# Moving the seven-product scheme from the w_out matmuls to the W matmuls, with W's blocks kept in DRAM

## Chip, cores, metric

One core of a Trainium2 chip. The metric is the device time of one execution in microseconds (us). Five engines run their own instruction queues in order: TensorE (PE; its weight loads are listed as PEld), VectorE (DVE), ScalarE (ACT), GpSimd (POOL) and SyncE (SP, which issues the DMAs here). "Wide" below means a matmul of 512 columns, "narrow" one of 256.

## What is computed

```python
# q, k, v: (4, 6080, 256); w_in: (256, 2048); w_out: (2048, 256)
qn = q / (norm(q, axis=1) + 1e-6);  kn = k / (norm(k, axis=1) + 1e-6)
s = kn.transpose(0, 2, 1) @ qn / tau          # 256 x 256 for each batch
a = softmax(s)                                # rows
x = (v @ a).reshape(24320, 256)
h = maximum(x @ w_in, 0)
out = h * h @ w_out
```

The kernel never forms x: for each batch b it makes W = a @ w_in (256 x 2048), and the output is relu(v W)^2 w_out. The inputs w_in and w_out are 64-bit floats.

## The kernel before

**Tiling.** Tokens of a batch are cut into NB = 12 blocks, ten of 512 and two of 480: 48 blocks in all, numbered (b, n). W has 2048 columns, NF = 16 slices of 128. A step is one block and one slice f; two steps are a pair (r = f // 2, part = f % 2), so a block is 8 pairs. `steps` lists them all; the first two blocks are interleaved by groups of four slices (the first PAIR = 32 steps), while weights are still decoded.

**Precision.** Every product of 32-bit numbers is made of three matmuls in a faster format: each operand is split into a high part (a cast on ACT) and a low part (a subtraction on DVE), and hi x hi, hi x lo, lo x hi are added in PSUM. So wo_hi/wo_lo hold w_out, w_hi/w_lo hold W, v_hi/v_lo a block of v, and g_hi/g_lo the squared activations.

**First product** (`first_product`, PSUM tile ps_h): for a step, 2 x 3 wide matmuls, v block by W slice, then a relu by ACT into x. It is the ordinary block product: for a pair, 12 wide matmuls, "eight products" of 2 x 2 blocks.

**Second product** (PSUM tile ps_o): from block 2 on, except for the last block, each pair uses a scheme of seven block products in place of eight (`seven_products`, 21 narrow matmuls for a pair, 9 in part 0 and 12 in part 1). It needs sums of the activations (`squares_and_sums`, on DVE), their hi and lo parts (`parts_of_sums`), sums of w_out's blocks (`sums_of_w_out`, once, tiles wS_hi/wS_lo), and at the end of a block `combine`, five DVE adds, and four output DMAs. Blocks 0, 1 and the last use `eight_products` (12 wide for a pair, evicted by ACT at the end of a block).

**The order.** The main loop runs over steps; at each it issues the first product of this step, pieces of the attention work, the square and splits of this pair or the one before, and the second product of the pair LAG = 2 pairs earlier. `InProgramOrder` keeps each engine's instructions in that order. The attention work of batches 1 to 3 is a generator (`attention`): 25 chunks of q and k a batch (five of batch 1 are done before), each split into hi and lo in one pair and multiplied into the Gram matrix in the next, then softmax, then W in four groups (`softmax_and_W`, PSUM tile ps_w). It is advanced once in each step, except in the steps f = 2 and 3. Group g of W for the next batch waits until the last block of this batch has used the old one (`may_write_W`), because W lives in SBUF (pool wpool, tags w_hi and w_lo, four buffers each, one for a group).

**PSUM.** ps_h has three buffers of one bank, ps_o two of two banks, the Gram matrix one bank.

**v.** A block of v is loaded by one DMA, cast to v_hi at f = 6 and subtracted to v_lo at f = 8 of the block before.

Of the kernel before, what the change touches and what calls it, by code (L numbers as in the profile page):

```python
# [30 lines left out]
def kernel(  # L31
# [36 lines left out]
    PPG = FPG // 2  # L68
    LAST = 3
# [44 lines left out]
    def decode(k, hi_lo, raw, shape, read):  # L114

        words = raw.bitcast(I32).rearrange("p a (b w) -> p a b w", w=2)  # L120
        low, high = words[:, :, :, 0], words[:, :, :, 1]
        E = pool.tile(shape, I32, tag=("qk_lo", "o_sb")[k % 2], name="dec_e", bufs=1)
        M = pool.tile(shape, I32, tag=("qk_hi", "dec")[k % 2], name="dec_m", bufs=1)
# [77 lines left out]
    def sums_of_w_out():  # L201
# [3 lines left out]
        for g in range(NG):  # L205
            fs, rs = slice(g * FPG, (g + 1) * FPG), slice(g * PPG, (g + 1) * PPG)
            w = pool.tile([P, FPG, C], F32, tag="qk_hi", name=f"wo{g}", bufs=1)
            S = pool.tile([P, 4, PPG, P], F32, tag="qk_lo", name=f"wo_sums{g}", bufs=1)
# [193 lines left out]
    def softmax_and_W(b):  # L402
# [41 lines left out]
        diag = pool.tile([P, NC, P], F32, tag="diag", name=f"diag{b}", bufs=1)  # L444
# [39 lines left out]
        for g in range(NG):  # L484
            while (b, g) not in may_write_W:
                yield
# [7 lines left out]
            w_hi = wpool.tile([P, NC, GRP], F32R, tag="w_hi", name=f"w_hi{b}_{g}")  # L494
            w_lo = wpool.tile([P, NC, GRP], F32R, tag="w_lo", name=f"w_lo{b}_{g}")
# [16 lines left out]
            def evict(h):  # L512
                ps = ps_w.pop(h)[:, 0:GRP]
                scalar.activation(w_hi[:, h, :], ps, AF.Copy, scale=rinv[:, h : h + 1])
# [9 lines left out]
            if b == 0:  # L524
# [3 lines left out]
                for h in range(NC):  # L528
                    evict(h)
            else:  # L530
                for h in range(NC):
# [5 lines left out]
                    yield  # L537
            W[b, g] = w_hi, w_lo
            yield
# [3 lines left out]
    may_write_W = {(0, g) for g in range(NG)}  # L543
    V = {}

# [6 lines left out]
    def split_v_hi(b, n):  # L552
        tn = blocks[n][1]
        V[b, n][1] = pool.tile([P, NC, T], F32R, tag="v_hi", name=f"v_hi{b}_{n}")
        scalar.copy(V[b, n][1][:, :, :tn], V[b, n][0][:, :, :tn])

# [4 lines left out]
    def split_v_lo(b, n):  # L561
        tn = blocks[n][1]
        raw, hi, _ = V[b, n]
        V[b, n][2] = pool.tile([P, NC, T], F32R, tag="v_lo", name=f"v_lo{b}_{n}")
        vector.tensor_sub(V[b, n][2][:, :, :tn], raw[:, :, :tn], hi[:, :, :tn].bitcast(F32))

    def by_seven(b, n):

        return (0, 1) < (b, n) < order[-1]

    X = {}
    G = {}

    def first_product(b, n, f):
        tn = blocks[n][1]
# [9 lines left out]
        if f % 2 == 0:  # L585
            X[b, n, f // 2] = pool.tile([P, 8, tn // 2], F32, tag="x", name=f"x{b}_{n}_{f // 2}")
        x = X[b, n, f // 2].rearrange("p s t -> p (s t)")
        s = slice((f % 2) * tn, (f % 2 + 1) * tn)
        scalar.activation(x[:, s], ps[:, :tn], AF.Relu)

    def parts_of(b, n, r):
        half = blocks[n][1] // 2
        shape = [P, 7 if by_seven(b, n) else 4, half]
        return [pool.tile(shape, F32R, tag=name, name=f"{name}{b}_{n}_{r}") for name in ("g_hi", "g_lo")]

    def squares_and_sums(b, n, r):

        x = X[b, n, r]  # L600
        G[b, n, r] = hi, lo = parts_of(b, n, r)
        scalar.activation(x[:, 0:4, :], x[:, 0:4, :], AF.Square)
        if by_seven(b, n):
            hi_, lo_, src = hi[:, 0:3, :], lo[:, 0:3, :], x[:, 1:4, :]
            vector.tensor_sub(x[:, 4:6, :], x[:, 1:3, :], x[:, 0:1, :].broadcast_to(list(x[:, 1:3, :].shape)))
            scalar.copy(hi_, src)
            vector.tensor_add(x[:, 6, :], x[:, 2, :], x[:, 4, :])
            vector.tensor_sub(x[:, 7, :], x[:, 3, :], x[:, 6, :])
            vector.tensor_sub(lo_, src, hi_.bitcast(F32))

    def parts_of_sums(b, n, r):

        x = X.pop((b, n, r))
        hi, lo = G[b, n, r]
        if by_seven(b, n):
            hi, lo, src = hi[:, 3:7, :], lo[:, 3:7, :], x[:, 4:8, :]
        else:
            src = x[:, 0:4, :]
# [5 lines left out]
    def second_product(b, n, r, part):  # L624
        if by_seven(b, n):
            seven_products(b, n, r, part)
        else:
            eight_products(b, n, r, part)

    def weights_of(r):  # L630

        out = {}
        for name, i, j in (("A11", 0, 0), ("A12", 0, 1), ("A22", 1, 1)):
            out[name] = [w[:, 2 * r + j, i * P : (i + 1) * P] for w in (wo_hi, wo_lo)]
        for i, name in enumerate(("S1n", "S2", "S3", "S4")):
            out[name] = [late[part][:, i, r, :] for part in ("hi", "lo")]
        return out


    SEVEN = (  # L640
        (None, ("A11", 0), ("A12", 2), ("S2", 5)),
        (("S1n", 3), ("S3", 4), ("S4", 1), ("A22", 6)),
    )

    def seven_products(b, n, r, part):
        t0, tn = blocks[n]
        half = tn // 2
        if r == 0:
            O[b, n, part] = ps_acc.tile([P, 4, T // 2], F32, tag="o", name=f"ps_o{b}_{n}_{part}")
        ps = O[b, n, part]  # L650
        hi, lo = G[b, n, r]
        w = weights_of(r)
        begun = set()
        for at, product in enumerate(SEVEN[part]):
            if product is None:
                continue
            w_hi, w_lo = w[product[0]]
            slot = product[1]
            for i, (wt, gt) in enumerate(((w_hi, hi), (w_hi, lo), (w_lo, hi))):
                tensor.matmul(  # L660
                    ps[:, at, :half],
                    wt,
                    gt[:, slot, :],
                    start=r == 0 and at // 2 not in begun,
                    stop=r == NPAIR - 1 and i == 2,
                    skip_group_check=True,
                )
                begun.add(at // 2)
        if part:
            del G[b, n, r]  # L670
        if r == NPAIR - 1:

            if part == 0:
                O[b, n] = pool.tile([P, 7, half], F32, tag="o_sb", name=f"o{b}_{n}", bufs=1)
            o, first = O[b, n], 1 - part
            scalar.copy(o[:, 3 * part : 3 * part + 4 - first, :], O.pop((b, n, part))[:, first:4, :half])
# [3 lines left out]
    def combine(b, n):  # L680
# [5 lines left out]
        vector.tensor_add(o[:, 1:3, :], o[:, 1:3, :], both(0))  # L686
        yield
        vector.tensor_add(o[:, 4, :], o[:, 4, :], o[:, 2, :])
        vector.tensor_add(o[:, 0, :], o[:, 4, :], o[:, 3, :])
        yield  # L690
        vector.tensor_add(o[:, 3, :], o[:, 3, :], o[:, 2, :])
        vector.tensor_add(o[:, 5:7, :], o[:, 5:7, :], o[:, 3:5, :])
        at = b * N + t0
        out = outT[:, at : at + tn].rearrange("(m p) t -> p m t", p=P)
        for m, k, slot in ((0, 0, 5), (0, 1, 1), (1, 0, 0), (1, 1, 6)):
# [5 lines left out]
    def eight_products(b, n, r, part):  # L701
# [4 lines left out]
        hi, lo = (x.rearrange("p s t -> p (s t)")[:, part * tn : (part + 1) * tn] for x in G[b, n, r])  # L706
# [73 lines left out]
    def then_sums():  # L780
        while grams[1].raws if B > 1 else False:
            yield
        yield from sums_of_w_out()

    sums = then_sums()
# [6 lines left out]
    LAG = 2  # L792
    beside = attention_of_others()
    for i in range(len(steps) + 2 * LAG):
        part = now["part"] = i % 2
        if i < len(steps):
# [3 lines left out]
            if n == NB - 1 and f % FPG == FPG - 1:  # L800
                may_write_W.add((b + 1, f // FPG))
# [3 lines left out]
        else:  # L805
# [5 lines left out]
            if i > 24:  # L811
# [16 lines left out]
        if i >= 2 * LAG:  # L828
            second_product(*pairs[i // 2 - LAG], part)
        if i < len(steps):  # L830
            at_hi, at_lo = (None, None) if at == 0 else (12, 13) if at == 1 else (6, 8)
            if i == 2 and len(order) > 2:
                load_v(*order[2])
            if f == at_hi and at + 1 < len(order):
                split_v_hi(*order[at + 1])
            if f == at_lo and at + 1 < len(order):
                split_v_lo(*order[at + 1])
                if at + 2 < len(order):
                    load_v(*order[at + 2])
        if i >= PAIR and part:  # L840
            for gen in gens:
                next(gen, None)

# [26 lines left out]
```

## Time and profile before

| | |
|---|---|
| median of 3 runs | 2222.92 us (2221.24 to 2222.95) |
| the profiled execution | 2223.07 us, span 2221.3 us |
| TensorE matmuls, busy | 2206.3 us (99%), 13740 instructions |
| ACT busy | 1845.8 us (83%) |
| DVE busy | 1761.8 us (79%) |
| DMA | 126.99 MB, mean 57 GB/s |
| granted TensorE clock | 0.999 |

The span is from the first to the last instruction on the core. A group line of the profile reads: line, engine, operation, output<-inputs with shapes, count | busy us, mean ns of one | idle time before it and who ended it. All helpers record one source line (L27), so instructions are told apart by tile names and shapes. A timeline line is start, duration, engine, operation, count of merged instructions, and in brackets the idle time before and who ended it. Matmul rows overlap each other, and their ends are modelled; the distance of starts is their pace.

### The profile page before, as it was taken

Reading aid. Unit: us, or ns where it says so; the run is one execution under the profiler, and the core shown is the slowest. Engines: PE = TensorE matmul, PEld = TensorE weight load, DVE = VectorE, ACT = ScalarE, POOL = GpSimd, SP = SyncE. Lnnn points to the kernel's source line nnn. Section 1 sums busy time; section 2 is a strip of 40 time slices with the busy share of each in tenths; the row PEclk is TensorE's granted clock in tenths of the full one; section 3 lists DMA queues with packets and bytes.
Section 4 is the critical chain, followed back from the end, with each engine's and each line's share of the span. In section 5 each row is a group of like instructions: output and inputs, shape, how many; then the busy total and the mean of one; then the engine's idle time right before and its main releaser. Section 6 shows DMA issues by size and latency. Waiting matters only on the chain.

```text
span 2221.3 us, 34359 instructions
## 1 busy us (share of the span) xinstructions
PE 2206.3 (99%) x13740; PEld 1980.9 (89%) x13740; DVE 1761.8 (79%) x2470; ACT 1845.8 (83%) x2294; POOL 0.7 (0%) x6
## 2 busy tenths in 40 slices
PE   8999999999999999999999999999999999999999
PEld 7788999989989999988998999998899888888898
DVE  7868888878778888878777888887877777787773
ACT  5788888888778888888878888888887888888885
POOL 0000000000000000000000000000000000000000
PEclk9999999999999999999999999999999999999999
DMA  9510122110211112110111122110102010010000
GB/s 341 178 67 29 60 69 70 47 38 25 70 66 58 60 60 72 62 41 22 36 67 56 60 66 75 58 53 22 33 25 76 21 36 20 22 37 20 22 26 18
DMA packets 76495, 126.99 MB, mean 57 GB/s; under 512 B 7728, under 2 KB 35120, under 8 KB 76336
## 3 DMA queue, kind: packets, MB, share of 16 engines
q1 hardware_dynamic: 76336, 124.81, 17.2%
q8 instruction: 107, 1.75, 0.3%
q14 instruction: 52, 0.43, 0.1%
HBM read 95.68 MB, written 29.10 MB: 56 GB/s over the span
## 4 chain that ended last, share of the span: by engine, by line
PE 95%; DVE 3%; DMA 1%; ACT 1%; issue 0%; SPq 0%; DVEq 0%; ACTq 0%
PE ps_h L27 46%; PE ps_o L27 41%; PE gram L27 5%; PE ps_w L27 2%; DVE g_lo L27 1%; DMA qk<-in_k 1%; DVE acc L27 1%; DVE x L27 0%; ACT x L27 0%; DMA qk<-in_q 0%; ACT g_hi L27 0%; PE ps_n L27 0%; DVE o L27 0%; DVE dec_m L27 0%; DVE wo_sums L27 0%
## 5 line engine op out<-in xcount | busy, mean ns | idle before, releaser
L27 DVE TENSOR_TENSOR g_lo<-x,g_hi 128x768 fp32r<-128x768 f32 (+2 forms) x744 | 804.5, 1081 | 96.2 <-ACT g_hi L27 95.7
L27 DVE TENSOR_TENSOR x<-x 128x256 f32<-128x256 f32 (+3 forms) x1080 | 551.4, 511 | 274.4 <-ACT x L27 249.3
L27 ACT CAST g_hi<-x 128x768 fp32r<-128x768 f32 (+2 forms) x744 | 697.7, 938 | 23.8 <-DVE x L27 10.5
L27 ACT ACTIVATE x<-ps_h 128x512 f32<-128x512 f32 (+1 forms) x768 | 456.7, 595 | 297.2 <-PE ps_h L27 277.3
L27 PE MATMUL ps_h<-v_hi,w_hi 128*128 128x512 f32 (+1 forms) x1536 | 478.8, 393 | 0.0
L27 PE MATMUL ps_h<-v_hi,w_lo 128*128 128x512 f32 (+1 forms) x1536 | 478.0, 392 | 0.0
L27 PE MATMUL ps_h<-v_lo,w_hi 128*128 128x512 f32 (+1 forms) x1536 | 475.2, 390 | 0.0
L27 ACT ACTIVATE x<-x 128x1024 f32<-128x1024 f32 (+1 forms) x384 | 404.6, 1054 | 11.9
L27 PE MATMUL ps_o<-g_lo,wS_hi 128*128 128x256 f32 (+1 forms) x1440 | 402.4, 279 | 3.0 <-DVE g_lo L27 2.8
L27 PE MATMUL ps_o<-g_hi,wS_lo 128*128 128x256 f32 (+1 forms) x1440 | 401.6, 279 | 0.0
L27 PE MATMUL ps_o<-g_hi,wS_hi 128*128 128x256 f32 (+1 forms) x1440 | 400.8, 278 | 0.0
L27 PEld LDWEIGHTS ps_h<-v_lo,w_hi 128*128 128x128 f32 x1536 | 288.1, 188 | 65.0
L27 PEld LDWEIGHTS ps_h<-v_hi,w_lo 128*128 128x128 f32 x1536 | 288.8, 188 | 62.1
L27 PE MATMUL ps_o<-g_hi,wo_hi 128*128 128x256 f32 (+3 forms) x1176 | 330.6, 288 | 1.0 <-ACT g_hi L27 1.0
L27 PE MATMUL ps_o<-g_hi,wo_lo 128*128 128x256 f32 (+3 forms) x1176 | 330.8, 288 | 0.0
L27 PE MATMUL ps_o<-g_lo,wo_hi 128*128 128x256 f32 (+3 forms) x1176 | 330.3, 287 | 0.1
L27 PEld LDWEIGHTS ps_o<-g_lo,wS_hi 128*128 128x128 f32 x1440 | 271.3, 188 | 19.6 <-DVE g_lo L27 3.8
L27 PEld LDWEIGHTS ps_o<-g_hi,wS_hi 128*128 128x128 f32 x1440 | 270.8, 188 | 15.5
L27 PEld LDWEIGHTS ps_o<-g_hi,wS_lo 128*128 128x128 f32 x1440 | 271.0, 188 | 0.0
L27 PEld LDWEIGHTS ps_h<-v_hi,w_hi 128*128 128x128 f32 x1536 | 239.0, 188 | 5.2
L27 PEld LDWEIGHTS ps_o<-g_hi,wo_hi 128*128 128x128 f32 x1176 | 221.5, 188 | 17.6 <-ACT g_hi L27 1.4
L27 PEld LDWEIGHTS ps_o<-g_lo,wo_hi 128*128 128x128 f32 x1176 | 220.8, 188 | 16.8 <-DVE g_lo L27 0.5
(87 smaller groups left out, 1667.9 us busy)
## 6 DMA issues: line engine op xcount, KB each, us to landing
qk<-in_k SPq DMA_DIRECT2D x87, 256.0 KB, 2.8
qk<-in_q SPq DMA_DIRECT2D x87, 256.0 KB, 3.0
v<-in_vT SPq DMA_DIRECT2D x40, 512.0 KB, 3.8
out_T<-o SPq DMA_DIRECT2D x152, 128.0 KB, 1.7
wi_hi<-wi_kept SPq DMA_DIRECT2D x12, 512.0 KB, 3.3
wi_lo<-wi_kept SPq DMA_DIRECT2D x12, 512.0 KB, 4.1
w_raw<-in_w_in SPq DMA_DIRECT2D x4, 1024.0 KB, 5.2
w_raw<-in_w_out SPq DMA_DIRECT2D x4, 1024.0 KB, 5.6
```

Of the source, the lines that this page charges most:

```text
L27: return lambda *args, **kwargs: self.tc.keep_in_program_order(issue(*args, **kwargs))
```

## The change

The seven-product scheme moves to the first product. From block 3 on (FIRST = 3) the product with W takes seven block products (`first_by_seven`), and the second product takes eight everywhere (BY_SEVEN is empty, so `some_by_seven` is false and `eight_products` runs for every block). Blocks 0 to 2 keep the ordinary first product.

`first_by_seven` holds two ps_h tiles, `one` and `two`, for a pair. In part 0 it makes four block products (12 narrow matmuls); then ACT copies `one` to SBUF, and DVE makes u, adds onto the halves `one[1]` and `two[1]` in PSUM, and makes c22. In part 1 three more block products (9 narrow) are accumulated onto `one[0]`, `one[1]` and `two[1]`, and ACT takes the relu of c22, `one` and `two[1]`. Squares and splits follow as in a block by eight; the sums on the activations, `combine` and its four DMAs are gone.

v's blocks are needed in sums too: `split_v_hi` (f = 9) and `split_v_lo` (f = 10) split three blocks of v, `sums_of_v` (f = 13) makes four sums on DVE and casts them on ACT, `parts_of_v_sums` (f = 14) makes their low part; the next v is loaded at f = 14.

W's blocks and their sums are made once a batch (`sums_of_W`; `keep_first_W` for batch 0, in the place of `sums_of_w_out`) and written to DRAM (W_kept, two sets, by b % 2). For each pair `load_W` reads the seven blocks, hi and lo, in two DMAs of 128 x 3584 bytes, AHEAD_W = 3 pairs ahead, into the buffers w_hi and w_lo. The wait may_write_W is gone.

```diff
+    BY_SEVEN = ()
+    FIRST_SEVEN = 4
...
-            while (b, g) not in may_write_W:
-                yield
...
+    def sums_of_W(b, g, w, parts=None):
+        v = w.rearrange("p j (r i m) -> p i j r m", r=PPG, i=2)
+        (A11, A12), (A21, A22) = [[v[:, i, j] for j in range(2)] for i in range(2)]
+        S = pool.tile([P, 4, PPG, P], F32, tag="qk", name=f"w_sums{b}_{g}", bufs=QK_BUFS)
+        S1, S2, S3, S4 = (S[:, i] for i in range(4))
+        vector.tensor_add(S1, A21, A22)
+        vector.tensor_sub(S3, A11, A21)
+        vector.tensor_sub(S2, S1, A11)
+        vector.tensor_sub(S4, A12, S2)
+        yield
+        if parts is None:
+            hi = pool.tile([P, NC, GRP], F32R, tag="qk_hi", name=f"w_hi{b}_{g}", bufs=1)
+            lo = w.bitcast(F32R)
+            scalar.copy(hi, w)
+            vector.tensor_sub(lo, w, hi.bitcast(F32))
             yield
+        else:
+            hi, lo = parts
+        S_hi = pool.tile([P, 4, PPG, P], F32R, tag="qk_lo", name=f"wS_hi{b}_{g}", bufs=1)
+        scalar.copy(S_hi, S)
+        vector.tensor_sub(S.bitcast(F32R), S, S_hi.bitcast(F32))
+        for i, (a, sums) in enumerate(((hi, S_hi), (lo, S))):
...
+                nc.sync.dma_start(kept[:, 0:2, :], a[:, 0, :, r, :])
+                nc.sync.dma_start(kept[:, 2, :], a[:, 1, 1, r, :])
+                nc.sync.dma_start(kept[:, 3:7, :], sums[:, :, r, :])
...
+    def load_W(b, r):
...
+        for part, kept in zip(parts, W_kept[b % 2][r]):
+            nc.sync.dma_start(part.bitcast(F32), kept)
...
+            V[b, n][1] = hi = pool.tile([P, 7, tn // 2], F32R, tag="v_hi", name=f"v_hi{b}_{n}")
+            scalar.copy(hi[:, 0, :], raw[:, 0, 0 : tn // 2])
+            scalar.copy(hi[:, 1:3, :].rearrange("p k t -> p (k t)"), raw[:, 1, :tn])
...
+    def sums_of_v(b, n):
...
+        vector.tensor_sub(T1, B12, B11)
+        vector.tensor_sub(T3, B22, B12)
+        vector.tensor_sub(T2, B22, T1)
+        vector.tensor_sub(T4n, B21, T2)
+        scalar.copy(hi[:, 3:7, :], S)
...
+        x = x_of(b, n, r)
+        if part == 0:
+            H[b, n, r] = one, two = [
+                ps_h.tile([P, 2, T // 2], F32, tag="h", name=f"ps_h{b}_{n}_{r}_{i}") for i in range(2)
+            ]
+            product(one[:, 0], 0, 0, True, False)
+            product(one[:, 1], 3, 3, False, False)
+            product(two[:, 0], 4, 4, True, False)
+            product(two[:, 1], 5, 5, False, False)
+            u, p1, p5, c22 = (x[:, i, :] for i in range(4))
+            scalar.copy(x[:, 1:3, :], one[:, :, :half])
+            vector.tensor_add(u, two[:, 0, :half], p1)
+            vector.tensor_add(one[:, 1, :half], u, p5)
+            vector.tensor_add(two[:, 1, :half], two[:, 1, :half], u)
+            vector.tensor_add(c22, two[:, 1, :half], p5)
+        else:
+            one, two = H.pop((b, n, r))
+            product(one[:, 0], 1, 1, False, True)
+            product(one[:, 1], 6, 2, False, True)
+            product(two[:, 1], 2, 6, False, True)
+            scalar.activation(x[:, 3, :], x[:, 3, :], AF.Relu)
+            scalar.activation(x[:, 0:2, :], one[:, :, :half], AF.Relu)
+            scalar.activation(x[:, 2, :], two[:, 1, :half], AF.Relu)
...
+            if part == 0 and at >= FIRST - 1:
+                ahead = at * NPAIR + f // 2 + AHEAD_W
+                if FIRST * NPAIR <= ahead < len(order) * NPAIR:
+                    load_W(order[ahead // NPAIR][0], ahead % NPAIR)
...
+            if at + 1 >= FIRST and at + 1 < len(order):
+                at_hi, at_lo = 9, 10
+                if f == 13:
+                    sums_of_v(*order[at + 1])
+                if f == 14:
+                    parts_of_v_sums(*order[at + 1])
+                    if at + 2 < len(order):
+                        load_v(*order[at + 2])
```

More of the change, by code (lines that the diff above doesn't have):

```diff
@@ L513, in evict @@
                 ps = ps_w.pop(h)[:, 0:GRP]
+                if b:
+                    scalar.activation(w[:, h, :], ps, AF.Copy, scale=rinv[:, h : h + 1])
+                    return
                 scalar.activation(w_hi[:, h, :], ps, AF.Copy, scale=rinv[:, h : h + 1])
@@ L529, in softmax_and_W @@
                     evict(h)
+                W[b, g] = w_hi, w_lo
+                yield
             else:
@@ new lines, with keep_first_W @@
+    done_W = set()
+    def keep_first_W():
+        for g in range(NG):
+            hi, lo = W[0, g]
+            w = pool.tile([P, NC, GRP], F32, tag="qk", name=f"w0_{g}", bufs=QK_BUFS)
+            vector.tensor_add(w, hi.bitcast(F32), lo.bitcast(F32))
+            yield
+            yield from sums_of_W(0, g, w, (hi, lo))
+    loaded = {}
+    def load_W(b, r):
+        assert (b, r // PPG) in done_W, (b, r)
+        loaded[b, r] = parts = [
+            wpool.tile([P, 7, P], F32R, tag=tag, name=f"{tag}{b}_{r}") for tag in ("w_hi", "w_lo")
+        ]
+        for part, kept in zip(parts, W_kept[b % 2][r]):
+            nc.sync.dma_start(part.bitcast(F32), kept)
@@ L544 @@
     V = {}
+    FIRST = 3
     def load_v(b, n, tag="v"):
@@ L562, in split_v_lo, with by_seven, some_by_seven, x_of @@
         tn = blocks[n][1]
[L563 to L569, printed above, removed]
+        raw, hi = V[b, n][:2]
+        if plain(b, n):
+            V[b, n][2] = pool.tile([P, NC, T], F32R, tag="v_lo", name=f"v_lo{b}_{n}")
+            vector.tensor_sub(V[b, n][2][:, :, :tn], raw[:, :, :tn], hi[:, :, :tn].bitcast(F32))
+        else:
+            V[b, n][2] = lo = pool.tile([P, 7, tn // 2], F32R, tag="v_lo", name=f"v_lo{b}_{n}")
+            vector.tensor_sub(lo[:, 0, :], raw[:, 0, 0 : tn // 2], hi[:, 0, :].bitcast(F32))
+            flat = lambda x: x[:, 1:3, :].rearrange("p k t -> p (k t)")
+            vector.tensor_sub(flat(lo), raw[:, 1, :tn], flat(hi).bitcast(F32))
+    def by_seven(b, n, r):
+        return (0, FIRST_SEVEN) <= (b, n) < order[-1] and r in BY_SEVEN
+    def some_by_seven(b, n):
+        return any(by_seven(b, n, r) for r in range(NPAIR))
     X = {}
+    XS = {}
     G = {}
+    def x_of(b, n, r):
+        if (b, n, r) not in X:
+            X[b, n, r] = pool.tile([P, 4, blocks[n][1] // 2], F32, tag="x", name=f"x{b}_{n}_{r}")
+        return X[b, n, r]
     def first_product(b, n, f):
+        if plain(b, n):
+            first_by_eight(b, n, f)
+        else:
+            first_by_seven(b, n, f // 2, f % 2)
+    def first_by_eight(b, n, f):
         tn = blocks[n][1]
@@ L598, in squares_and_sums @@
     def squares_and_sums(b, n, r):
         x = X[b, n, r]
[L601 to L609, printed above, removed]
+        shape = [P, 4, blocks[n][1] // 2]
@@ new lines, in squares_and_sums @@
+        G[b, n, r] = [pool.tile(shape, F32R, tag=name, name=f"{name}{b}_{n}_{r}") for name in ("g_hi", "g_lo")]
+        hi, lo = G[b, n, r]
+        scalar.activation(x, x, AF.Square)
+        if by_seven(b, n, r):
+            hi, lo, src = hi[:, 1:4, :], lo[:, 1:4, :], x[:, 1:4, :]
+            XS[b, n, r] = xs = pool.tile(shape, F32, tag="xs", name=f"xs{b}_{n}_{r}", bufs=1)
+            vector.tensor_sub(xs[:, 0:2, :], x[:, 1:3, :], x[:, 0:1, :].broadcast_to(list(x[:, 1:3, :].shape)))
+            scalar.copy(hi, src)
+            vector.tensor_add(xs[:, 2, :], x[:, 2, :], xs[:, 0, :])
+            vector.tensor_sub(xs[:, 3, :], x[:, 3, :], xs[:, 2, :])
+            vector.tensor_sub(lo, src, hi.bitcast(F32))
@@ L622, with second_product @@
     O = {}
[L624 to L627, printed above, removed]
+    def second_product(b, n, r, part, ahead):
+        if some_by_seven(b, n):
+            products_of_pair(b, n, r, part, ahead)
+        elif not ahead:
             eight_products(b, n, r, part)
@@ L632, in weights_of @@
         out = {}
[L633 to L636, printed above, removed]
+        for i in range(2):
+            for j in range(2):
+                out[f"A{i + 1}{j + 1}"] = [w[:, 2 * r + j, i * P : (i + 1) * P] for w in (wo_hi, wo_lo)]
+        if late:
+            for i, name in enumerate(("S1n", "S2", "S3", "S4")):
+                out[name] = [late[part][:, i, r, :] for part in ("hi", "lo")]
@@ L654, in seven_products @@
[L654 to L658, printed above, removed]
-            for i, (wt, gt) in enumerate(((w_hi, hi), (w_hi, lo), (w_lo, hi))):
[L660 to L668, printed above, removed]
+        for place, name, slot in mine:
+            ps = O[b, n, part][:, place % 4, :half]
+            w_hi, w_lo = w[name]
+            hi, lo = (x[:, slot % 4, :] for x in g[2 * (slot // 4) :][:2])
+            for i, (wt, gt) in enumerate(((w_hi, hi), (w_hi, lo), (w_lo, hi))):
+                bank = b, n, place // 2
+                tensor.matmul(ps, wt, gt, start=bank not in begun, stop=r == NPAIR - 1 and i == 2, skip_group_check=True)
+                begun.add(bank)
@@ L669, in seven_products @@
+        if ahead:
+            return
         if part:
@@ L673, in seven_products @@
             if part == 0:
[L674 to L676 removed]
+                O[b, n] = pool.tile([P, 8, half], F32, tag="o_sb", name=f"o{b}_{n}", bufs=1)
+            scalar.copy(O[b, n][:, 4 * part : 4 * part + 4, :], O.pop((b, n, part))[:, :, :half])
             if part:
@@ L792 @@
     LAG = 2
+    AHEAD_W = 3
     beside = attention_of_others()
@@ L795 @@
         part = now["part"] = i % 2
+        if part and i >= 2 * LAG:
+            second_product(*pairs[i // 2 - LAG], part, True)
         if i < len(steps):
@@ L828 @@
         if i >= 2 * LAG:
-            second_product(*pairs[i // 2 - LAG], part)
+            second_product(*pairs[i // 2 - LAG], part, False)
         if i < len(steps):
@@ L842 @@
                 next(gen, None)
+        if 40 < i < 64 and part and BY_SEVEN:
+            next(late_sums, None)
 def kernel(**inputs):
```

136 lines of the change are left out of this document (93 added, 43 removed).

## The prediction

> **What bounds the kernel now.** I read the page from the top, the list of waits, one pair of steps in the timeline, and the groups of instructions by form for the durations.
>
> ```profile
> span 2221.3 us, 34359 instructions
> PE 2206.3 (99%) x13740; PEld 1980.9 (89%) x13740; DVE 1761.8 (79%) x2470; ACT 1845.8 (83%) x2294; POOL 0.7 (0%) x6
> PE 95%; DVE 3%; DMA 1%; ACT 1%; issue 0%; SPq 0%; DVEq 0%; ACTq 0%
> PE ps_o L27 <- DVE g_lo L27: 2.8, 2, 1.9
> PE ps_o L27 <- ACT g_hi L27: 1.0, 1, 1.0
> ```
>
> TensorE is the chain (95%), and it waited some 4 us for ACT and DVE in the products. So the stream of matmuls sets the time. The pace of that stream, from the timeline (start, duration, engine):
>
> ```profile
> 1900.17 0.63 PE L27 MATMUL ps_h<-v_hi,w_hi 128*128 128x512 f32 x2
> ...
> 1901.10 0.63 PE L27 MATMUL ps_h<-v_hi,w_lo 128*128 128x512 f32 x2
> 1901.57 0.28 PE L27 MATMUL ps_o<-g_hi,wo_hi 128*128 128x256 f32 x1
> 1901.76 0.60 ACT L27 ACTIVATE x<-ps_h 128x512 f32<-128x512 f32 x1 [0.20 <-PE ps_h L27]
> 1902.62 0.62 PE L27 MATMUL ps_h<-v_hi,w_hi 128*128 128x512 f32 x2
> 1904.01 0.28 PE L27 MATMUL ps_o<-g_hi,wS_hi 128*128 128x256 f32 x1
> 1905.40 0.63 PE L27 MATMUL ps_h<-v_hi,w_hi 128*128 128x512 f32 x2
> ```
>
> Six wide matmuls (512 columns) take 1901.57-1900.17 = 1.40 us, nine narrow ones (256) 1902.62-1901.57 = 1.05, six wide 1.39, twelve narrow 1.39: 5.23 us for a pair, 0.233 a wide one and 0.1165 a narrow one; rows of 0.28 and 0.4 overlap. The last wide matmul of the third line starts at 1901.33, ends by the model 0.40 later, and ACT starts at 1901.76: 0.03 us from a product to its reader.
>
> **The matmuls: equal.** A pair of before is 12 wide (product with W) and 21 narrow (w_out). After, it is 21 narrow (W) and 12 wide (w_out): 5.23 us again, for 45 blocks of 48 in both, with LAG the same. Block 2 loses the seven: 8 x (12 x 0.233 - 21 x 0.1165) = +2.8 us; the last block gains it with 480 columns: 8 x that x 480/512 = -2.6. Sum +0.2.
>
> **What moves into TensorE's way.** Before, nothing of ACT or DVE stood between two products of one pair but a relu; squares, sums and splits had LAG = 2 pairs of time. Now the pair goes A0 (12 narrow, part 0), S0 (six wide of w_out), A1 (9 narrow, which accumulate onto what DVE has written in PSUM), S1 (six wide). Between A0 and A1 lie: copy of `one` on ACT, then on DVE u, `one[1]`, `two[1]`, c22. The seventh matmul of A1, the first that adds to `two[1]` must wait for c22, which reads it. The cover is S0 and the first six matmuls of A1. Durations (mean ns after the bar's busy time) and waits:
>
> ```profile
> L27 ACT COPY o<-ps_o 128x512 f32<-128x512 f32 x4 | 2.1, 582 | 0.0
> L27 ACT ACTIVATE x<-ps_h 128x512 f32<-128x512 f32 x640 | 383.6, 599 | 230.0 <-PE ps_h L27 216.2 <-DVE g_lo L27 5.2 <-DVE v_lo L27 2.0
> L27 ACT ACTIVATE x<-x 128x1024 f32<-128x1024 f32 x320 | 340.1, 1063 | 9.8
> L27 ACT CAST g_hi<-x 128x1024 fp32r<-128x1024 f32 x320 | 335.3, 1048 | 10.4 <-DVE x L27 9.3
> L27 ACT CAST g_hi<-x 128x768 fp32r<-128x768 f32 x304 | 254.2, 836 | 10.1 <-PE ps_o L27 0.4
> L27 DVE TENSOR_TENSOR x<-x 128x256 f32<-128x256 f32 x608 | 258.6, 425 | 20.8
> L27 DVE TENSOR_TENSOR eT_lo<-ps_t,eT_hi 128x512 fp32r<-128x512 f32 x4 | 2.8, 692 | 0.1
> L27 DVE TENSOR_TENSOR acc<-acc 128x512 f32<-128x512 f32 x4 | 2.7, 686 | 0.0
> L27 DVE SCALAR_TENSOR_TENSOR w_lo<-ps_w,rinv,w_hi 128x512 fp32r<-128x512 f32 x32 | 23.6, 747 | 5.6 <-ACT w_hi L27 5.5
> 704.16 0.60 ACT L27 ACTIVATE x<-ps_h 128x512 f32<-128x512 f32 x1 [0.96 <-PE ps_h L27]
> 704.66 1.04 ACT L27 CAST qk_hi<-qk 128x1024 fp32r<-128x1024 f32 x1
> 705.60 1.05 ACT L27 CAST g_hi<-x 128x1024 fp32r<-128x1024 f32 x1
> 700.09 1.22 DVE L27 TENSOR_TENSOR acc<-acc,qk 128x1024 f32<-128x1024 f32 x1
> 701.22 1.22 DVE L27 TENSOR_TENSOR g_lo<-x,g_hi 128x1024 fp32r<-128x1024 f32 x1
> 1900.73 1.61 DVE L27 TENSOR_TENSOR x<-x 128x512 f32<-128x512 f32 x3 [1.05 <-ACT x L27]
> 186.24 1.22 DVE L27 TENSOR_TENSOR g_lo<-x,g_hi 128x1024 fp32r<-128x1024 f32 x1
> 187.51 0.39 PE L27 MATMUL ps_o<-g_lo,wS_hi 128*128 128x256 f32 x1 [0.96 <-DVE g_lo L27]
> 187.51 0.19 PEld L27 LDWEIGHTS ps_o<-g_lo,wS_hi 128*128 128x128 f32 x1 [1.16 <-DVE g_lo L27]
> ```
>
> Three readings. Independent instructions overlap by about 0.1 us on ACT (704.16 to 704.66 for a row of 0.60, then 0.94 for one of 1.04) and 0.09 on DVE (1.13 for 1.22); three dependent ones (0.69, then 0.425 twice) take 1.61, so a dependent one follows 0.034 after. An ACT row costs 1048-836 = 212 ns per 256 columns, so 0.41 us for 256 from SBUF and 599-212 = 0.39 from PSUM. After DVE's end (187.46) TensorE starts at 187.51, and it is the weight load that waits, which otherwise goes one matmul ahead: a late operand is late 0.05 + 0.115 us before its matmul's turn. For DVE on PSUM there are read rows (692 against 686 in SBUF; 747 with a scalar operand) and none that writes: per add I bound the extra between -0.05 us (1.61's gaps vanish) and 0.06 (747-692), and take 0, by the nearest row, the 692 one.
>
> Pair without attention beside it, zero at A0's start: `one` is complete at 5 x 0.1165 + 0.28 + 0.03 = 0.89, `two` at 1.59. Copy 0.89-1.47. u waits for both halves of `two`, which share a bank: 1.59; then `one[1]` 2.05, `two[1]` 2.39 (independent of the second), c22 2.85 to 3.27; with 0.05 it is 3.32. A1 starts at 2.80, the weight load of its seventh matmul is due at 2.80 + 5 x 0.1165 = 3.38. **Slack 0.06 us** for c22 and 0.15 for the end of the copy. The Trainium skill ("PSUM — Partial Sum Buffer", § PSUM bank collisions) has two engines in one bank at once as an error; no run here shows it, and without that wait u would start 0.09 earlier.
>
> ACT then has the cast of the pair before (1.37-2.42), relu c22 (3.30-3.71), `one` (3.72-4.32), `two` (to 4.60), the square (to 5.70); the next copy is due at 5.23 + 0.89 = 6.12. ACT's idle is then about 0.5 us a pair, less than any of the three block-wide jobs that the loop queues there, in odd steps right before the next copy:
> - f = 3: eviction of the block's output, two copies from 5.61 to 6.69; the next copy 6.59-7.17, u 0.38 late, less 0.06: 0.32 us of stall.
> - f = 9: v's two hi casts (0.41, 0.62) to 6.54; copy from 6.45 to 7.03: u 0.23 late, stall 0.17.
> - f = 13: DVE's four v sums follow g_lo (3.18-4.40): 4.31, 4.65, 4.98, 5.44-5.87; ACT's cast of them 5.90-6.95, copy 6.85-7.43, u 0.64 late: stall 0.58.
>
> Before, the like jobs (v_hi cast, evictions, combine) delayed only relus that had two pairs to spare. Sum **1.07 us a block**.
>
> With attention's Gram products beside it, pairs alternate between a split (ACT cast and DVE subtract, 1.05 and 1.22 more, no matmuls) and products (a square, an add and 12 narrow matmuls, six of them before S0, so 0.70 more cover). By the same working the copy stays on time in either. Blocks alternate too, as 7 of 8 pairs advance the generator: in one kind only the f = 13 job shows (v sums end at 6.95, cast 8.03, copy 8.51 against a u due at 6.63+1.59 = 8.22: 0.23); in the other f = 3 costs 0.32 and f = 13, with the copy ending 8.51 against 6.82 and 0.70 cover, 0.93. Mean 0.74. How many blocks:
>
> ```profile
> L27 DVE TENSOR_TENSOR qk_lo<-qk,qk_hi 128x1024 fp32r<-128x1024 f32 x64 | 78.3, 1224 | 27.2 <-ACT qk_hi L27 26.0
> q1 hardware_dynamic: 76336, 124.81, 17.2%
> wi_hi<-wi_kept SPq DMA_DIRECT2D x12, 512.0 KB, 3.3
> wi_lo<-wi_kept SPq DMA_DIRECT2D x12, 512.0 KB, 4.1
> GB/s 341 178 67 29 60 69 70 47 38 25 70 66 58 60 60 72 62 41 22 36 67 56 60 66 75 58 53 22 33 25 76 21 36 20 22 37 20 22 26 18
> ```
>
> 64 full chunks (and by the program 6 short ones), two pairs each, 7 pairs a block: 20 blocks. 25 others. Stalls: 20 x 0.74 + 25 x 1.07 = 14.8 + 26.8 = **41.6 us**.
>
> **The rest of the edit.** W's sums for the first batch replace those of w_out with the same instructions (add of 1024, four of 256, cast, subtract): 0. For 12 later groups ACT has two casts (1.05) and DVE four adds of 256 and two subtracts of 1224 ns instead of two of 747; they lie in pairs of which two of three have six wide ps_w matmuls as extra cover (1.40 us); of a third pair I take 0.2 us: **2.4**. Without that cover 12 x 1 us. combine() leaves DVE (five adds a block): 0, nothing waited for it. The wait for the batch's last block goes, so attention runs earlier; the same matmuls, 0. Loads of W: 2 x 128 x 3584 B = 0.92 MB a pair, 0.92/5.23 us = 175 GB/s beside a mean of 57, against 341 in the first slice; they are issued three pairs (15.7 us) ahead, into a buffer freed a step before, and 512 KB lands in 3.3 to 4.1: 0, unless the queue is blocked for 10 us. On SP's queue they stand behind q, k loads and stores that wait for DVE some 5 us; 720 loads more, some 100 output stores fewer, 48 stores of W a batch. End of the kernel: one relu and the adds more after the last product: 0.5.
>
> Sum, against this execution's 2223.07 us (span 2221.3 and 1.8 around it; the runs' median is 2222.92): 41.6 + 2.4 + 0.2 + 0.5 = 44.7, so 2268 us.
>
> **The rivals.**
> - *Every pair waits.* If an add with PSUM operands takes 0.06 longer (the 747 row), c22 comes 4 x 0.06 = 0.24 later: slack -0.18. The 290 or so pairs without extra cover (360 less 70 product pairs) pay 0.18: 52; the events' slack of 0.06 goes: 45 x 2 x 0.06 = 5 more. 2268 + 57 = 2325. Against it: the 692 row. The Trainium skill ("Perfetto Trace Analysis", § Optimizing Scalar/DVE Operations) gives DVE about 60 ns of access overhead in SBUF and 125 in PSUM; by that the sum would be this rival's, an estimate of 0.26 us a pair, but the read rows of this trace do not show the difference.
> - *No stall (the other side).* If adds hand over at the independent pace (0.335 instead of 0.459 for two hand-overs: 0.25) and the wait sits on the matmul, not its weight load (0.115), slack is 0.43; f = 13 still shows: 25 x 0.21, and 10 x (1.69 - 0.70 - 0.43) in the second kind of Gram block, 11 us: 2223 + 11 = 2234. It decides from a slack of 0.8, where 10 x 0.2 = 2 us are left: 2225 us. ACT would have to run the copy ahead of the block-wide jobs. For it: ACT and DVE have idle time (83%, 79%), so the jobs could be done elsewhere. Against: 1.61 for three adds, the waiting weight load at 187.51, and the class that keeps program order on each engine.
> - *W comes late.* If a load lands over 15.7 us after its issue, each pair pays the rest: at 1 us, 2268 + 360 = 2628. Against: 232 GB/s in all, of the 341 shown.
>
> **How the numbers follow.** Stalls once a block 0.58; every pair 0.28; none 0.10; late loads 0.04. Within 0.2% (4.4 us, about what a measurement can tell from no change) lies most of the third: same 0.07, faster 0.03 (nothing here removes matmuls; only the 4 us of waits could go), slower 0.90. The forecast's own range is 2240 to 2300. The range asked for reaches into the rival of every pair, up to an extra of 0.1 us an add (slack -0.34, 290 x 0.34 = 99): 2232 to 2360.
>
> **What would show it.** TensorE's pace inside A0, S0, A1, S1 unchanged; waits of ps_h's weight loads for DVE's c22, about two or three a block (100 to 130), 0.2 to 0.9 us each, behind output copies, v_hi casts and the cast of v's sums on ACT; adds of 256 at 0.425. If DVE's rows with PSUM are at 0.48 or more and waits number 300, the rival of every pair holds. If W's loads land late, waits name the DMA. The prediction is wrong if ACT's order differs from the program's as I lined it up, or if a buffer of ps_h (two of three held by a pair) comes free later than the relu of `one` at 4.32 against its need at 5.23 + 0.70.

## The result, and the profile after

The changed kernel takes 2313.11 us (median of 4, 2312.37 to 2314.64) against 2222.93: a ratio of 1.0408 (95% interval 1.0395 to 1.0421), 4.1% slower. The profiled execution has a span of 2311.2 us, 89.9 more than before's 2221.3. The forecast was slower by 45 us; it is slower by 90.

The page of the changed kernel (engines, the chain's shares by engine), and from its list of waits the largest of TensorE's first product for another engine (engine and output that waited, for whom, us in total, times, longest):

```profile
span 2311.2 us, 36972 instructions
PE 2254.8 (98%) x13740; PEld 1977.4 (86%) x13740; DVE 1490.6 (64%) x2563; ACT 1794.2 (78%) x2768; POOL 0.7 (0%) x6
PE 75%; DVE 14%; ACT 5%; DMA 3%; issue 2%; SPq 1%; DVEq 0%; ACTq 0%
PEld ps_h L27 <- ACT g_hi L27: 33.2, 63, 2.1
PEld ps_h L27 <- DVE v_lo L27: 17.6, 22, 1.4
PE ps_h L27 <- DVE v_lo L27: 13.1, 22, 1.2
PEld ps_h L27 <- ACT wS_hi L27: 11.4, 11, 1.9
PE ps_h L27 <- DVE ps_h L27: 11.1, 15, 1.6
```

The count of matmuls is the same 13740; DVE and ACT do less work than before, and yet TensorE's share of the chain fell from 95% to 75%, with 14% DVE and 5% ACT in it. These waits of the first product are new. A matmul and the weight load before it each have a row for the same wait, so these rows overlap and are not to be added.

The groups by form give the durations on which the prediction's schedule stood:

```profile
L27 DVE TENSOR_TENSOR x<-ps_h,x 128x256 f32<-128x256 f32 x592 | 251.5, 425 | 596.7 <-PE ps_h L27 378.3 <-ACT x L27 208.3
L27 DVE TENSOR_TENSOR ps_h<-x 128x256 f32<-128x256 f32 x296 | 128.1, 433 | 10.2
L27 DVE TENSOR_TENSOR ps_h<-ps_h,x 128x256 f32<-128x256 f32 x296 | 126.0, 426 | 0.0
L27 ACT COPY x<-ps_h 128x512 f32<-128x512 f32 x296 | 173.5, 586 | 150.0 <-PE ps_h L27 148.8 <-DVE nu L27 0.5 <-DVE ns L27 0.5
```

An add with an operand or its result in PSUM takes 0.425 to 0.433 us, as taken (0.425); the copy 0.586 (0.582).

From the starts of all 13740 matmuls I took the distance of each from the one before, less the pace (0.1175 us after a matmul of 256 columns, 0.2329 after 512, 0.1115 after 240, 0.2175 after 480), and summed the excess over each pair's A0 and A1, with the start that follows A1. Means over blocks, in us, by the pair r:

```
changed kernel                       r=0   r=1   r=2   r=3   r=4   r=5   r=6   r=7
9 blocks without attention (36-44)
  A0                                0.05  0.01  0.01  0.02  0.01  0.01  0.02  0.01
  A1                                0.03  0.03  0.27  0.01  0.02  0.14  0.01  0.62
8 blocks with Gram products (even)
  A0                                1.20  0.01  0.01  0.01  0.01  0.01  0.01  0.01
  A1                                0.01  0.03  0.27  0.01  0.01  0.01  0.01  0.98
7 blocks with Gram products (odd)
  A0                                0.47  0.01  0.01  0.01  0.01  0.01  0.01  0.01
  A1                                0.02  0.01  0.01  0.01  0.01  0.01  0.01  0.35
11 blocks with softmax or W: 33.1 us in all, 3.0 a block
all 45 blocks: 87.5 us
```

The ten blocks that fit none of these kinds hold the other 15 us. So 87.5 of the 89.9 us are waits inside A0 and A1, nearly all at a few fixed places. One of them, r = 7 of a block without attention, in the timeline (ACT, then DVE, then TensorE):

```profile
1910.83 1.05 ACT L27 CAST v_hi<-v_sums 128x1024 fp32r<-128x1024 f32 x1 [0.26 <-DVE v_sums L27]
1911.78 0.58 ACT L27 COPY x<-ps_h 128x512 f32<-128x512 f32 x1
1912.39 0.42 DVE L27 TENSOR_TENSOR x<-ps_h,x 128x256 f32<-128x256 f32 x1 [1.60 <-ACT x L27]
1912.85 0.43 DVE L27 TENSOR_TENSOR ps_h<-x 128x256 f32<-128x256 f32 x1
1912.46 0.62 PE L27 MATMUL ps_o<-g_lo,wo_hi 128*128 128x512 f32 x2
1913.43 0.36 PE L27 MATMUL ps_h<-v_hi,w_hi 128*128 128x256 f32 x1 [0.35 <-ACT g_hi L27]
1913.40 0.19 PEld L27 LDWEIGHTS ps_h<-v_hi,w_hi 128*128 128x128 f32 x1 [0.74 <-ACT g_hi L27]
```

Before pair r = 7, ACT's cast of v's sums stands ahead of the copy, DVE waits 1.60 us for the copy, and TensorE, done with S0, waits to begin A1. The row names ACT's g_hi cast, which happened to end last (1913.31); the weight load's start stands 0.12 us after the end of the add to `one[1]` (1912.85 + 0.43 = 1913.28). That distance is no accident of this pair: in 301 of the 360 pairs the first weight load of A1 starts 0.11 to 0.12 us after that add's end (median 0.115).

Waits at r = 0, which the prediction did not have, look like this (DVE, then TensorE):

```profile
640.11 1.21 DVE L27 TENSOR_TENSOR qk_lo<-qk,qk_hi 128x1024 fp32r<-128x1024 f32 x1
641.24 1.15 DVE L27 TENSOR_TENSOR g_lo<-x,g_hi 128x960 fp32r<-128x960 f32 x1
642.31 1.22 DVE L27 TENSOR_TENSOR v_lo<-v_sums,v_hi 128x1024 fp32r<-128x1024 f32 x1
642.35 0.28 PE L27 MATMUL ps_h<-v_hi,w_hi 128*128 128x256 f32 x1
643.59 0.39 PE L27 MATMUL ps_h<-v_lo,w_hi 128*128 128x256 f32 x1 [0.96 <-DVE v_lo L27]
```

The low part of v's sums, issued at f = 14 behind attention's qk_lo and g_lo, ends at 643.53; the fifth matmul of the next block's first pair needs it at 642.47.

### The profile page after: what moved, and what is told of

The parts are those of the page before. It is cut to its first block, busy times and chain, and to the rows that moved or that the text cites. A ratio compares the mean times of both kernels' runs of the same rounds, so it can differ in the third digit from the quotient of the medians.

```text
span 2311.2 us, 36972 instructions
## 1 busy us (share of the span) xinstructions
PE 2254.8 (98%) x13740; PEld 1977.4 (86%) x13740; DVE 1490.6 (64%) x2563; ACT 1794.2 (78%) x2768; POOL 0.7 (0%) x6
## 4 chain that ended last, share of the span: by engine, by line
PE 75%; DVE 14%; ACT 5%; DMA 3%; issue 2%; SPq 1%; DVEq 0%; ACTq 0%
PE ps_h L27 35%; PE ps_o L27 35%; PE gram L27 3%; DVE g_lo L27 3%; DVE x L27 2%; DVE ps_h L27 2%; DVE v_sums L27 2%; PE ps_w L27 2%; ACT x L27 2%; DVE acc L27 2%; ACT v_hi L27 1%; DVE v_lo L27 1%; DMA w_lo<-W_kept 1%; DVE qk_lo L27 1%; ACT g_hi L27 1%
## 5 line engine op out<-in xcount | busy, mean ns | idle before, releaser
L27 PE MATMUL ps_h<-v_hi,w_hi 128*128 128x256 f32 (+2 forms) x2616 | 752.9, 291 | 31.3 <-DVE ps_h L27 11.1
L27 PE MATMUL ps_h<-v_lo,w_hi 128*128 128x256 f32 (+2 forms) x2616 | 739.0, 285 | 13.1 <-DVE v_lo L27 13.1
L27 PE MATMUL ps_h<-v_hi,w_lo 128*128 128x256 f32 (+2 forms) x2616 | 738.0, 285 | 0.0
L27 ACT ACTIVATE x<-x 128x256 f32<-128x256 f32 (+2 forms) x744 | 554.2, 745 | 201.8 <-DVE x L27 187.8
L27 PE MATMUL ps_o<-g_hi,wo_lo 128*128 128x512 f32 (+1 forms) x1536 | 481.0, 394 | 0.0
L27 PE MATMUL ps_o<-g_hi,wo_hi 128*128 128x512 f32 (+1 forms) x1536 | 477.9, 392 | 0.9 <-ACT g_hi L27 0.9
L27 PE MATMUL ps_o<-g_lo,wo_hi 128*128 128x512 f32 (+1 forms) x1536 | 477.2, 392 | 0.1
L27 DVE TENSOR_TENSOR g_lo<-x,g_hi 128x1024 fp32r<-128x1024 f32 (+1 forms) x384 | 463.2, 1206 | 15.5 <-ACT g_hi L27 15.3
L27 ACT CAST g_hi<-x 128x1024 fp32r<-128x1024 f32 (+1 forms) x384 | 399.4, 1040 | 0.0
L27 ACT ACTIVATE x<-ps_h 128x512 f32<-128x512 f32 (+3 forms) x768 | 340.3, 492 | 63.7 <-PE ps_h L27 62.5
```

The lines of the kernel that those rows point to most:

```text
L27: return lambda *args, **kwargs: self.tc.keep_in_program_order(issue(*args, **kwargs))
```

## The experiments

Two theories stood: (1) ACT and DVE jobs stand in their queues in front of the copy and the adds of the next pair, or make v_lo late; (2) the DMA of W, or a chain that is too long in every pair.

**W's loads.** W is loaded for four pairs a batch, and these blocks are used for all pairs; the kernel leaves out the loads of the other 344 pairs, so its products take the wrong blocks of W.

```diff
-                    load_W(order[ahead // NPAIR][0], ahead % NPAIR)
+                    bl, bn = order[ahead // NPAIR]
+                    if ahead < FIRST * NPAIR + 4 or (bn == 0 and ahead % NPAIR < 4):
+                        load_W(bl, ahead % NPAIR)
+                        held[ahead % NPAIR] = loaded[bl, ahead % NPAIR]
+                    else:
+                        loaded[bl, ahead % NPAIR] = held[ahead % 4]
```

> W is loaded for the first four pairs of each batch only, and these blocks are used for all others (so the products use the wrong blocks of W); 340 of 360 pairs have no load. Theory: the loads are hidden, 0 to 5 us off, 2308 to 2313, same waits at r = 0, 2 and 7. Rival (330 MB more of DMA slow the engines' accesses or come late): 25 us or more off, and shorter rows on ACT and DVE or a narrow matmul's pace nearer 0.1165 us.

Measured 2312.28 us, 0.8 less than the changed kernel. DMA of the changed kernel and of this one:

```profile
q1 hardware_dynamic: 226752, 484.52, 62.6%
w_hi<-W_kept SPq DMA_DIRECT2D x360, 448.0 KB, 3.5
w_lo<-W_kept SPq DMA_DIRECT2D x360, 448.0 KB, 4.3
```

```profile
q1 hardware_dynamic: 127680, 168.86, 22.8%
PEld ps_h L27 <- ACT g_hi L27: 33.2, 63, 2.1
PEld ps_h L27 <- DVE v_lo L27: 17.6, 22, 1.4
```

With 484.5 MB down to 168.9 these waits are the same to 0.1 us, and those of A0 and A1 add up to 87.3 us against 87.5. The loads of W cost nothing that can be seen; that rival falls. The stores of W are in both runs; they come back below, under the W stage.

**v's jobs moved.** ACT's casts go, in four pieces, behind the cast of g_hi in even steps, where ACT waits for c22 anyway; DVE's jobs to f = 5, 9 and 13.

```diff
-                at_hi, at_lo = 9, 10
-                if f == 13:
-                    sums_of_v(*order[at + 1])
-                if f == 14:
-                    parts_of_v_sums(*order[at + 1])
...
+                at_hi, at_lo = None, 9
+                nxt = order[at + 1]
+                if f in (2, 8):
+                    split_v_hi(*nxt, piece=f // 8)
+                if f == 5:
+                    sums_of_v(*nxt)
+                if f in (10, 12):
+                    cast_v_sums(*nxt, f // 2 - 5)
+                if f == 13:
+                    parts_of_v_sums(*nxt)
```

> v's jobs go to other places: ACT's casts into even steps behind the cast of g_hi, in four pieces (f = 2, 8, 10, 12), the four DVE sums to f = 5, the low parts to f = 9 and 13. Theory (TensorE waits for ACT and DVE jobs that stand in front of the next pair's copy and adds, or make v_lo late): the waits in front of the first products of r = 0 (20.5 us in all) and r = 7 (27.9) and those of f = 9 (about 3) go: 50 us off 2313, 2258 to 2268, and the waits for v_lo are gone. Rival (ACT and DVE have no room, the work only delays another pair): under 25 us off, with the waits at r = 2 to 6 in their place. Rival (the time is in W's loads or in slower matmuls): no change within 5 us.

Measured 2266.22 us: 47 off, within the expected. The waits at r = 0 fell from 20.5 us (A0, all blocks) to 0.6 and those at r = 7 from 27.9 (A1) to 1.3; the v_lo rows are gone. Half of the loss was v's jobs, by their place in the queues (the cast of the sums, besides, goes in two halves); no work was taken out.

**Only v_lo of the sums.** The same subtraction, issued at the start of step f = 14.

```diff
+            if f == 14 and at + 1 >= FIRST and at + 1 < len(order):
+                parts_of_v_sums(*order[at + 1])
+
         if i >= PAIR:
             gens = (beside,)
...
-                    parts_of_v_sums(*order[at + 1])
```

> Only the subtraction that makes the low part of v's sums moves, in its step f = 14, ahead of the attention work and of g_lo on DVE; v's casts and sums stay at f = 9 and 13. Theory: the waits for v_lo in front of r = 0 (20 us) go, those at r = 7 (28) stay: 15 to 21 us off 2313, 2292 to 2298. Rival (g_lo or the attention's low part is late in its place, or ACT's cast of the sums was the cause): under 6 us off.

Measured 2296.02 us: 17 off. In A0 of r = 0 the excess fell to 0.5 us, while r = 7 kept its 27.9. So the late v_lo is a cost of its own, besides that of the cast of the sums.

**Output copies moved** to the ends of the even steps f = 4 and 6, one each.

```diff
+            if not last:
+                late_out.append((o, out, psum, tn))
+                return
...
+        if late_out and part == 0:
+            evict_late(late_state[0])
+            late_state[0] ^= 1
```

> The two output copies of a block, in the odd step f = 3 before, go one each to the ends of the even steps f = 4 and 6. Theory: the wait at r = 2 (9.8 us in 45 blocks) goes: 8 to 12 us off, 2301 to 2305. Rival (only moved): within 3 us of 2313, with waits of the same size at r = 3 or 4.

Measured 2304.16 us: 9 off; the excess at r = 2 fell from 9.8 to 1.1 us.

**The W stage.** The first try waited for an even step only before the cast of W's sums.

```diff
+        if b:
+            yield from until_even()
         S_hi = pool.tile([P, 4, PPG, P], F32R, tag="qk_lo", name=f"wS_hi{b}_{g}", bufs=1)
```

> One wait for the next even step more in the generator before ACT's cast of W's sums, so that it does not stand in front of the next pair's copy. Theory: the 11 waits of a weight load on that cast (11.4 us) go: 7 to 13 us off, 2300 to 2306. Rival (another job of the W stage is late next): within 3 us of 2313.

Measured 2312.8 us, no change, and the same waits. The cast that the list names stood in an even step already; the one that hurts is w to w_hi in an odd one, as the changed kernel's timeline shows:

```profile
545.59 1.03 ACT L27 CAST w_hi<-w 128x1024 fp32r<-128x1024 f32 x1
546.53 0.55 ACT L27 COPY x<-ps_h 128x480 f32<-128x480 f32 x1
546.65 1.23 DVE L27 TENSOR_TENSOR w<-w,w_hi 128x1024 fp32r<-128x1024 f32 x1 [0.69 <-ACT w_hi L27]
547.80 0.40 DVE L27 TENSOR_TENSOR x<-ps_h,x 128x240 f32<-128x240 f32 x1
548.79 0.35 PE L27 MATMUL ps_h<-v_hi,w_hi 128*128 128x240 f32 x1 [0.60 <-DVE ps_h L27]
```

The cast comes before the copy, and the subtraction that needs it (1.23 us) comes before the adds: A1 starts at 548.79. The second try moves that cast and the subtraction too, and puts four steps between a batch's first q, k loads and their first use.

```diff
+        if b > 1:
+            for _ in range(4):
+                yield
...
         yield
+        if b:
+            yield from until_even()
         if parts is None:
...
             yield
+            yield from until_even()
```

> Only the W stage's edits of the three: ACT's cast of w to hi waits for an even step (it stood in odd steps, in front of the next pair's copy), the cast of the sums too, and four steps lie between the first q, k loads of batches 2 and 3 and their first cast. Theory (what the three edits together gave beyond v's and the outputs' 56 us is this: 16 us): 12 to 19 us off 2313, 2294 to 2301, with the waits of r = 0, 2 and 7 left in plain blocks and blocks of Gram products. Rival (it paid only in company of the others): under 8 us off.

Measured 2300.5 us: 13 off, inside the expected range (the changed kernel beside it: 2313.68). In the eleven blocks with softmax or W the excess fell from 33.1 to 20.4 us; in the others it rose by some 2 us, to 77.1 in all.

A good part of the 13 us is one wait, in block 11 (ACT, DVE, TensorE of the changed kernel):

```profile
626.83 1.04 ACT L27 CAST qk_hi<-qk 128x1024 fp32r<-128x1024 f32 x1 [5.37 <-issue]
627.90 1.23 DVE L27 TENSOR_TENSOR qk_lo<-qk,qk_hi 128x1024 fp32r<-128x1024 f32 x1 [4.79 <-DMA qk<-in_k]
629.58 0.38 PE L27 MATMUL ps_h<-v_hi,w_hi 128*128 128x240 f32 x1 [3.83 <-ACT x L27]
```

The first q, k load of batch 2 was issued at 622.21, behind twelve stores of W on SP's queue (615.17 to 621.5). ACT stood 5.37 us for it, and the relus that free a ps_h buffer stood behind its cast. After the wait the matmuls ran at half their pace for some 3.5 us: the granted clock was 0.51 from 630.0 to 633.5, 1.00 before the wait and after 633.5. From 625.47 to 633.93, 8.46 us passed for 19 matmuls that take 2.79 at the usual pace: 5.7 us. In the run with the W stage's edits this wait is gone, so about 5.7 of the 13 us are the late q, k load, and the rest is the net of the moved casts.

> The changed kernel once more, on the same chip as the run beside it, to size that difference: 2311 to 2315.

Measured 2313.68 us, within the expected and 0.6 above the first measurement.

**The three together.**

> Three edits together: v's jobs moved (2266 alone), output copies moved (2304 alone), and in the W stage ACT's cast of w into even steps too, with four steps between the first q, k loads of a batch and their first cast. Theory: the gains add (47 + 9), and of the 25 us or so that wait in the softmax and W stages some 10 go: 2240 to 2256. Rival (moved jobs meet each other): above 2262.

Measured 2241.25 us, ratio to before 1.0087 (1.0070 to 1.0104): 72 off, about as the parts add up (47 + 9 + 13 = 69). Its page and its largest waits of first products:

```profile
PE 2227.6 (99%) x13740; PEld 1974.3 (88%) x13740; DVE 1489.7 (67%) x2563; ACT 1796.4 (80%) x2813; POOL 0.7 (0%) x6
PE 96%; DMA 1%; DVE 1%; ACT 1%; issue 0%; SPq 0%; DVEq 0%; ACTq 0%
PEld ps_h L27 <- issue: 38.4, 236, 0.5
PEld ps_h L27 <- ACT w_hi L27: 2.9, 9, 0.8
```

TensorE is the chain again (96%), and 17.3 us of excess are left in A0 and A1, against 18.5 us that it is slower than before (2222.8 beside it). With the same matmuls there was nothing to gain, only waits to lose. The 236 waits of weight loads for "issue" (0.16 us in the mean) have no releaser in the profile; in 292 pairs of this run the first weight load of A1 starts 0.11 to 0.12 us after the add to `one[1]`, so it does not go a matmul ahead as others do.

**The chain one add longer.** The first add is made twice.

```diff
             vector.tensor_add(u, two[:, 0, :half], p1)
+            vector.tensor_add(u, two[:, 0, :half], p1)
```

> The first of DVE's four adds in a pair is made twice (same result), so the chain between the two parts of a pair is one add of 256 longer, 0.335 to 0.459 us. Theory (the chain has no slack in a pair without extra cover, slack 0.06 at most): 290 pairs pay about 0.3: 85 to 125 us more, 2398 to 2438. Rival (slack of 0.3 or more, only the block-wide jobs reach TensorE): under 45 us more, below 2358.

Measured 2458.06 us: 145 more, above the expected range. The two adds follow each other as dependent ones (the same output), so the chain grew by 0.46, not by 0.335:

```profile
1901.04 0.88 DVE L27 TENSOR_TENSOR x<-ps_h,x 128x256 f32<-128x256 f32 x2 [2.66 <-ACT x L27]
1901.96 0.43 DVE L27 TENSOR_TENSOR ps_h<-x 128x256 f32<-128x256 f32 x1
1902.54 0.36 PE L27 MATMUL ps_h<-v_hi,w_hi 128*128 128x256 f32 x1 [0.50 <-DVE ps_h L27]
PE ps_h L27 <- DVE ps_h L27: 113.6, 290, 2.1
```

By the starts of the matmuls, 298 of the 360 pairs lost 0.4 us or more against the changed kernel (most 0.42 to 0.48, 13 of them 0.6 to 0.9), and 60 lost nothing, nearly all of them pairs with Gram products between their two parts. So a pair without that extra cover has no slack: whatever makes its adds later is a wait of TensorE in full. The expected range had taken 0.3 a pair.

**Seven products in both** for r = 1 and 7, with the three edits, as a version that could beat both. The cast of three squares goes behind the other casts of its step, and the copy of the output's second half to a later even step (lines not printed here).

```diff
-    BY_SEVEN = ()
+    BY_SEVEN = (1, 7)
...
```

> The three edits and the seven-product scheme in the second product too, for two of eight pairs (r = 1 and 7) of blocks 4 to 46; the cast of three squares stands behind the other casts of its step. TensorE saves 0.35 us in 86 pairs, 30 us. Theory: ACT's and DVE's idle time takes the sums, a third of the gain is lost to jobs in front of copies: 2220 to 2238, about the kernel of before. Rival (ACT has no room): 2247 or more.

Measured 2344.28 us, far above the theory's range. Two new waits stand out, of TensorE and of DVE; the first alone took more than the 30 us:

```profile
PEld ps_o L27 <- ACT o L27: 91.7, 43, 2.5
DVE xs L27 <- ACT x L27: 132.9, 86, 2.5
1912.37 0.69 DVE L27 TENSOR_TENSOR xs<-x 128x512 f32<-128x512 f32 x1 [1.68 <-ACT x L27]
1913.10 0.88 DVE L27 TENSOR_TENSOR xs<-x,xs 128x256 f32<-128x256 f32 x2
1913.90 0.42 DVE L27 TENSOR_TENSOR x<-ps_h,x 128x256 f32<-128x256 f32 x1
```

43 times, once a block, TensorE waited some 2 us for the copy of the output's second half, by the list of waits because it frees a PSUM buffer too late; and the sums of the squares stand on DVE ahead of the next pair's first add (1913.90). After 21 of these 43 waits, 13 to 17 matmuls ran at about half their pace, 32 us in all; the granted clock of this run is 0.985 in the mean, and 0.60 from 1733.7 to 1738 after one of them. No run takes the two waits apart. No version here beats the kernel of before.

## Why the prediction went as it did

The sign, the mechanism and three of its terms held; the size was half of the truth, because the low part of v's sums was left out and the W stage was priced too low.

- *Matmuls equal:* right. 13740 in both, and with the waits taken out the time is that of before to 1 us (18.5 us slower, 17.3 in waits).
- *Slack of a pair:* right in size (0.06 us predicted, none by the doubled add), wrong in place. It is not the seventh matmul of A1 that holds TensorE up, but the first, which adds to `one[0]` while DVE still writes `one[1]` in the same bank. The size held in part by luck: the seventh's weight load does wait for c22 (in 295 pairs it starts 0.05 us after it), but no more than 0.03 us behind the pace that the late first one has set, so both ends come out alike. The Trainium skill's rule against two engines in one bank ("PSUM — Partial Sum Buffer", § PSUM bank collisions raise a hardware error) was applied to u and not to this matmul; the traces agree that it waits, and none shows what a collision would do.
- *f = 3, 9 and 13 in blocks without attention:* 0.32, 0.17 and 0.58 us predicted, 0.27, 0.14 and 0.62 measured. In Gram blocks 0.23 and 0.93 for f = 13, measured 0.35 and 0.98.
- *The step that failed first:* the list of block-wide jobs ended at "any of the three block-wide jobs"; the fourth, `parts_of_v_sums` at f = 14, was left out. It delays no copy, but it is itself an operand of the next block's fifth matmul. Without attention it comes in time (0.05); in Gram blocks, behind qk_lo and g_lo on DVE, it costs 1.20 and 0.47 by turns: 20.5 us in all, 17 when moved alone.
- *The second:* "two of three have six wide ps_w matmuls as extra cover", with 0.2 us for the third pair, 2.4 us for the W stage. The third pair has ACT's cast and DVE's subtraction both ahead of the next chain, and pays 0.9 to 1.8 us. Blocks with softmax or W lost 33.1 us, 3.0 each against 1.07 taken and 2.4 in all; the W stage's edits took 13 us off. Some 5.7 of them belong to a term put at 0: the prediction asked whether W's loads come late behind others on SP's queue, and not whether a q, k load comes late behind W's stores, as it did once in block 11. That wait also showed one of the prediction's own signs of being wrong, a ps_h buffer that comes free late. Where the rest of the 33.1 us beyond the forecast went was not taken apart.
- *The rivals:* adds in PSUM are no slower by the row (0.425 to 0.433), and pairs that no other job disturbs lose 0.01 to 0.03 us in A1, not 0.18. Here the Trainium skill's larger overhead for DVE in PSUM ("Perfetto Trace Analysis", § Optimizing Scalar/DVE Operations) and the trace differ, and the measurement decides for this instruction. Late loads of W fell by the run without them, and "no stall" by the 87.5 us of waits.

## What to carry to other kernels

Before moving work into the path between two products, count the slack of one step from its start to its next use, and then list every job of every other engine's queue by two questions: what does it stand in front of, and who needs its own result first. Once the slack is gone, a rare job in an in-order queue costs the bounding engine whatever of its length the idle time before it does not take (0.14 to 1.2 us a time here, for jobs of 1.0 to 1.2 us), however idle the other engines are on average; the same jobs in a place where their engine waits anyway cost next to nothing (47 and 9 us came back here, and 13 in the W stage, with no work removed).

## What the runs showed of the hardware

An add of 256 columns takes the same time on DVE with operands and result in SBUF or in PSUM (0.425 against 0.425 to 0.433 us). A weight load that waits for a DVE add into PSUM starts 0.115 us after the add's end in the median of the changed kernel's 360 pairs (0.11 to 0.12 in 301 of them); one that waits for a DVE result in SBUF starts 0.05 us after it (187.51 before; the seventh load of A1 after c22, 0.052 to 0.053 in the median pair). And 316 MB of DMA more or less, at 211 and 74 GB/s in the mean, left the engines' work as it was (busy PE 2254.8 and 2254.4 us, DVE 1490.6 and 1489.6, ACT 1794.2 and 1794.5).

After a wait of 4.0 us in the middle of the kernel TensorE's granted clock was 0.51 for the next 3.5 us (630.0 to 633.5), and 1.00 on both sides of that stretch, so a stall can cost more than its length: 1.5 us more here. It does not follow each stall. In the run with seven products in both, 21 of 43 waits of 1.4 to 2.5 us were followed by such a stretch and 22 were not, waits of 2.06 us among either; what decides it stays open.
